# Scores and first mixing of a talking-heads attention as 64x32 TensorE tiles, with a new table of steps and two alternating orders of a step

## The chip, the cores and the metric

The kernel runs on one core of a Trainium2 chip. The metric is the device time of one execution in microseconds (us). The clock that TensorE was granted in the profiled execution was 0.994 of full speed on average.

## What is computed

Everything is 32-bit float. A batch of 8, 12 heads, 448 positions, 64 numbers a head. The scores of all heads are mixed by a 12x12 matrix before the softmax and mixed again by another one after it; then a Fourier mix and a feed-forward block of width 768 and 3072 follow.

```python
def _attn_ref(q, k, v, w_pre, w_post):
    scores = scale * np.matmul(q, k.transpose(0, 1, 3, 2))
    scores = np.einsum('bhij,hg->bgij', scores, w_pre)
    scores = scores - np.max(scores, axis=-1, keepdims=True)
    attn = np.exp(scores)
    attn = attn / (np.sum(attn, axis=-1, keepdims=True) + 1e-09)
    attn = np.einsum('bhij,hg->bgij', attn, w_post)
    return np.matmul(attn, v)

def _moe_ref(x, w_ch1, w_ch2):          # x: heads side by side, (8, 448, 768)
    u = x + np.real(np.fft.fft(np.fft.fft(x, axis=1), axis=2))
    un = (u - mean(u)) / np.sqrt(var(u) + 1e-06)
    return u + np.maximum(un @ w_ch1, 0.0) @ w_ch2
```

## The kernel before

There are two stages. `mix_phase` does attention and the Fourier mix, batch by batch, in about the first 812 us; `ffn_phase` does the feed-forward block, a seven-product scheme of half-size matrices, in the rest. The weights of the feed-forward block arrive as 64-bit floats and are turned into 32-bit ones on VectorE by a chain of small instructions (lines 229 to 261, "conversions" here). One such instruction is dealt out per step of the attention loop by `wts.deal(1)`.

The attention loop has 24 steps a batch, 192 in all. Step s does the second half of the work for row group T = s and the first half for T = s + 2 (`LM`), and fetches for T = s + 4 (`LG`). The pieces:

- **Scores** (`emit_qk`, L443). For 56 rows twice (`Sb` holds 124 rows), two heads at a time by x, two half blocks by y. A matmul takes 64 rows of q transposed as weights, 64x64 tiles, and streams 448 columns of k. Results lie in `ms` tiles of PSUM and are copied to `Sb` by ScalarE (L324). There are four `ms` buffers, which the other pieces use too.
- **Gather** (`emit_gather`, L459). Four DMAs on the SP queue bring the 12 heads of 5 rows onto 60 partitions, `Kr`, three buffers.
- **First mixing** (`emit_premix`, L469). Four matmuls, 60 rows by 64 columns of weights `kw1`, 448 columns streamed, into `mx`: two tiles, one buffer each.
- **Maximum and exponential** (`emit_max` L477 on VectorE, `emit_exp` L485 on ScalarE), each once for x = 0 and once for x = 1. The exponential also sums into `den`.
- **Scaling** (`emit_scale`). VectorE makes the reciprocal `rcp` (L493, L494), GpSimd multiplies `PP` by it (L496).
- **Second mixing** (`emit_postmix`, L506). Eight matmuls in 64x32 tiles, 448 columns, into `po`, one buffer; `emit_turn` (L517) transposes it on VectorE into `Pv`.
- **Second product** (`emit_av`, L533). 28 matmuls in 64x64 tiles with `v`, 120 columns; results are copied to `XT` by ScalarE.
- **The 128-wide blocks** ("full" in the code). Transposition of q and k (`emit_xpose`, L420; evicted to `qT` and `kT`), of `XT` (`emit_x`, L566), and the two products of the Fourier mix (`emit_z` L631, `emit_s2` L647, which updates `X` on VectorE, L658 and L660). Between them GpSimd does additions, the "folds" (L587 to L608).

In a 32-bit matmul TensorE makes two passes, so that each matmul above is two MATMUL and two LDWEIGHTS records in the profile.

The order on TensorE, VectorE, ScalarE and GpSimd is written by hand. For each step the loop at the end of `mix_phase` emits the pieces in one fixed order: first mixing, eviction of what is pending (`flush`), second mixing, maxima, exponentials, the second product if one is due, transposition of `po`, a conversion, scores if due, gather, scaling, deferred stores and folds, 128-wide blocks if due. When a piece falls due is in tables: `AT_T` for q's and k's transpositions, `AT_QK` scores, `AT_AV` second products, `AT_X`, `AT_Z`, `AT_S` the other 128-wide ones. `ENG` says which engine evicts what ("a" ScalarE, "d" VectorE). DMAs on SP follow as semaphores allow.

Of the kernel before, what the change touches and what calls it, by code (L numbers as in the profile page):

```python
# [10 lines left out]
F32 = mybir.dt.float32  # L11
# [65 lines left out]
AT_T = ((12, 10), (17, 16), (14, 18))  # L77
AT_L = ((-4, -3), (-2, -1), (0, 1), (2, 8), (12, 13), (14, 15))
AT_V = ((3, 4), (5, 6), (7, 7))
AT_QK = ((1, 2, 2), (0, 1, 2), (0, 1, 2), (0, 1, 2),  # L80
         (0, 1, 2), (0, 1, 2), (0, 1, 2), (0, 1, 2))
AT_AV = ((0, 2, 3), (1, 3, 5), (3, 4, 5), (1, 2, 3))
AT_X = (11, 20, 24, 29)
AT_Z = (38, 38, 41, 41)
AT_S = ((40, 44), (53, 55))

ENG = {("tr", "q", 4): "d", ("tr", "q", 3): "a", ("tr", "k", 4): "d",
       ("tr", "k", 3): "a", "QK": "aa", "AV": "aa", "X": "aa", "z": "a"}
# [196 lines left out]
def mix_phase(ctx, tc, rest, ident, q, k, v, w_pre, w_post, u_scr, u_rev, wts):  # L285
# [40 lines left out]
    def flush():  # L326
        while pend:
            pend.pop(0)[1]()
# [103 lines left out]
    def emit_qk(n, xx):  # L432
# [7 lines left out]
        for y in range(2):  # L440
            lo = r0 + MG * y
            for x in range(2):
                nc.tensor.matmul(  # L443
                    pss[x][64 * y:64 * y + r0 + 64 - lo, :S],
                    st["qT", xx][64 * x:64 * x + 64, y, lo:r0 + 64],
                    st["kT", xx][64 * x:64 * x + 64, y, :],
                    start=True, stop=True)
# [16 lines left out]
    def emit_premix(T):  # L464
        mx = [pmx.tile([P, 512], F32, name="mx", tag=f"mx{x}") for x in range(2)]
        Kr = steps[T]["Kr"]
        for x in range(2):
            for z in range(2):
                nc.tensor.matmul(mx[x][64 * z:64 * z + 64, :S],  # L469
                                 kw1[64 * x:64 * x + KR, :],  # L470
                                 Kr[64 * x:64 * x + KR, z, :], start=True, stop=True)
        steps[T]["mx"] = mx

    def emit_max(T):
        nmx = [psm.tile([P, 1], F32, name="nmx", tag=f"nmx{x}") for x in range(2)]
        for x in range(2):
            nc.vector.tensor_reduce(nmx[x][:, :], steps[T]["mx"][x][:, :S],  # L477
                                    axis=AX.X, op=ALU.max, negate=True)
        steps[T]["nmx"] = nmx

    def emit_exp(T):
        PP = ppp.tile([P, 2, S], F32, name="PP", tag="PP")
        den = psm.tile([P, 2], F32, name="den", tag="den")
        for x in range(2):
            nc.scalar.activation(PP[:, x, :], steps[T]["mx"][x][:, :S], ACTF.Exp,  # L485
                                 bias=steps[T]["nmx"][x][:, :],
                                 accum_out=den[:, x:x + 1])
        steps[T]["PP"], steps[T]["den"] = PP, den
# [260 lines left out]
    with tc.manual_schedule(engines={ET.PE, ET.DVE, ET.Activation, ET.Pool}):  # L749
        while s <= TOT - GS + AT_X[-1]:  # L750
            old = len(later)
            n = take("none", s)
            if 0 <= s + LM < TOT:
                emit_premix(s + LM)
            flush()
            if 0 <= s < TOT:
                emit_postmix(s)
            if 0 <= s + LM < TOT:
                emit_max(s + LM)
                emit_exp(s + LM)  # L760
            take("AV", s)
            if 0 <= s < TOT:
                emit_turn(s)
            if s >= 4:
                wts.deal(1)
            take("QK", s)
            if 0 <= s + LG < TOT:
                if any(e[2] is not None and e[2] <= (s + LG) // BS for e in pend):
                    flush()
                emit_gather(s + LG)  # L770
            if 0 <= s + LM < TOT:
                emit_scale(s + LM)
            for _ in range(old):
                later.pop(0)()
            for _ in range(min(len(folds), 1 if n and s > 3 else 2)):
                folds.pop(0)()
            take("full", s)
# [344 lines left out]
```

## Time and profile before

| what | us |
|---|---|
| median of 6 runs (2423.2 to 2429.62) | 2424.76 |
| the profiled execution | 2423.69 |
| its span, from the first to the last instruction | 2421.9 |

Busy time of the engines inside the attention stage, in two stretches of 100 us:

| from, to (us) | TensorE | VectorE | ScalarE | GpSimd |
|---|---|---|---|---|
| 100 to 200 | 99.9 | 77.4 | 73.4 | 81.2 |
| 600 to 700 | 98.2 | 78.3 | 67.8 | 73.8 |

Groups of instructions of the attention stage (line, engine, operation, tiles, shape, count; busy us, mean ns of one; idle time of the engine just before, and what ended most of it):

```profile
L469 PE MATMUL mx<-Kr,kw 60*64 60x448 f32 x1536 | 221.3, 553 | 6.5 <-DMA Kr<-Sb 4.6
L506 PE MATMUL po<-PP,kw 60*32 60x448 f32 x3072 | 188.7, 548 | 1.6 <-DVE rcp L493 1.6
L443 PE MATMUL ms<-kT,qT 64*64 64x448 f32 (+1 forms) x1536 | 189.4, 553 | 0.0
L477 DVE TENSOR_REDUCE nmx<-mx 128x1 f32<-128x448 f32 x384 | 222.3, 618 | 125.2 <-PE mx L469 123.0
L485 ACT ACTIVATE PP<-mx,nmx 128x448 f32<-128x448 f32 x384 | 240.0, 630 | 168.4 <-DVE nmx L477 156.2
L496 POOL TENSOR_SCALAR PP<-PP,rcp 128x448 f32<-128x448 f32 x384 | 240.6, 635 | 234.8 <-DVE rcp L494 101.7
```

The busy time of such a group is the union of its instructions' time, since several small tiles work side by side in TensorE: 1536 times 553 ns is 849 us, and 221.3 us of the span have such a matmul in them. In names like `60*64` the first number is the rows of the weights and the second the columns. The ends of matmuls are modelled, their starts are recorded; so distances are measured from start to start.

### The profile page before, as it was taken

What the parts mean: (1) busy time and instruction counts of PE and PEld (TensorE: products, weight loads), DVE (VectorE), ACT (ScalarE), POOL (GpSimd) and SP (SyncE); (2) the same over time, 40 slices, a digit from 0 to 9 for tenths busy, and PEclk for the clock granted to TensorE, in tenths of its full rate; (3) what the DMA queues carried; (4) which work ended last, traced back from release to release, by engine and by line L of the source; (5) the groups of instructions that cost most, each with busy time, mean ns of one, the idle gap of its engine ahead of it and who ended that gap; (6) DMA issues with size and microseconds to landing.
All of it is one profiled execution on the core that took longest, in us unless ns stands there. A gap on an engine that the chain in (4) does not pass through costs nothing.

```text
span 2421.9 us, 48510 instructions
## 1 busy us (share of the span) xinstructions
PE 2379.2 (98%) x18608; PEld 1553.3 (64%) x18608; DVE 1506.6 (62%) x3103; ACT 798.4 (33%) x2059; POOL 780.8 (32%) x1293
## 2 busy tenths in 40 slices
PE   7999999999999899999999999999999999999999
PEld 2445454454555477776777777777777777777776
DVE  3777778788787647785567356635665457533333
ACT  4777667676667542322111111111111110111110
POOL 3587877868676531120111011101110011000000
PEclk8999999999999999999999999999999999999999
DMA  6555554656554456346444444534442534343331
GB/s 151 176 182 160 179 171 155 197 161 194 165 164 147 163 199 215 126 149 234 145 137 153 143 147 134 159 116 168 145 149 98 200 127 146 121 169 112 118 117 53
DMA packets 168596, 372.10 MB, mean 154 GB/s; under 512 B 36750, under 2 KB 90022, under 8 KB 168366
## 3 DMA queue, kind: packets, MB, share of 16 engines
q1 hardware_dynamic: 129038, 260.22, 31.9%
q0 software_dynamic: 33760, 107.40, 14.9%
q8 instruction: 149, 2.44, 0.4%
q10 hardware_dynamic: 5568, 1.38, 0.3%
q14 instruction: 81, 0.66, 0.1%
HBM read 211.98 MB, written 74.34 MB: 118 GB/s over the span
## 4 chain that ended last, share of the span: by engine, by line
PE 94%; DMA 2%; SPq 1%; DVE 1%; ACT 1%; issue 0%; ACTq 0%; DVEq 0%
PE psP L946 18%; PE psP L1002 18%; PE psR L946 9%; PE psR L1002 9%; PE mx L469 7%; PE po L506 6%; PE ms L533 6%; PE ms L443 6%; PE psQ L1002 5%; PE psQ L946 4%; PE ms L647 2%; PE ms L420 2%; DMA Kr<-Sb 1%; PE ms L631 1%; SPq L459 1%; PE ms L566 1%
## 5 line engine op out<-in xcount | busy, mean ns | idle before, releaser
L946 PE MATMUL psP<-ub,w1t 128*128 128x256 f32 x2016 | 462.5, 379 | 0.0
L1002 PE MATMUL psP<-w2t,h 128*128 128x384 f32 x1344 | 460.9, 486 | 0.0
L946 PEld LDWEIGHTS psP<-ub,w1t 128*128 128x128 f32 x2016 | 382.8, 190 | 60.7
L207 POOL DMA_DIRECT2D raw<-in_moe_w_ch_dram x120 | 68.9, 574 | 924.5 <-DVE tmp L251 905.7
L1002 PEld LDWEIGHTS psP<-w2t,h 128*128 128x128 f32 x1344 | 254.4, 190 | 165.9
L496 POOL TENSOR_SCALAR PP<-PP,rcp 128x448 f32<-128x448 f32 x384 | 240.6, 635 | 234.8 <-DVE rcp L494 101.7
L477 DVE TENSOR_REDUCE nmx<-mx 128x1 f32<-128x448 f32 x384 | 222.3, 618 | 125.2 <-PE mx L469 123.0
L485 ACT ACTIVATE PP<-mx,nmx 128x448 f32<-128x448 f32 x384 | 240.0, 630 | 168.4 <-DVE nmx L477 156.2
L951 ACT COPY h<-psP 128x512 f32<-128x512 f32 x42 | 24.6, 585 | 764.4 <-PE psP L946 753.2
L1008 DVE TENSOR_TENSOR u<-u,psP 128x384 f32<-128x384 f32 x336 | 183.5, 552 | 141.3 <-PE psP L1002 139.2
L946 PE MATMUL psR<-ub,w1t 128*128 128x256 f32 x1008 | 231.3, 379 | 0.0
L1002 PE MATMUL psR<-w2t,h 128*128 128x384 f32 x672 | 230.5, 486 | 0.0
L469 PE MATMUL mx<-Kr,kw 60*64 60x448 f32 x1536 | 221.3, 553 | 6.5 <-DMA Kr<-Sb 4.6
L517 DVE STREAM_TRANSPOSE Pv<-po 128x896 f32<-128x896 f32 x192 | 212.8, 1108 | 15.6 <-PE po L506 13.2
L957 DVE TENSOR_TENSOR h<-h,psQ 128x512 f32<-128x512 f32 x42 | 28.9, 688 | 298.8 <-PE psQ L946 298.6
L946 PEld LDWEIGHTS psR<-ub,w1t 128*128 128x128 f32 x1008 | 191.4, 190 | 25.9
L324 ACT COPY Sb<-ms 124x448 f32<-124x448 f32 x384 | 184.7, 539 | 17.2 <-PE ms L631 5.1
L506 PE MATMUL po<-PP,kw 60*32 60x448 f32 x3072 | 188.7, 548 | 1.6 <-DVE rcp L493 1.6
L533 PEld LDWEIGHTS ms<-Pv,vv 64*64 64x64 f32 x5376 | 144.7, 133 | 70.1 <-issue 33.1
L443 PE MATMUL ms<-kT,qT 64*64 64x448 f32 (+1 forms) x1536 | 189.4, 553 | 0.0
L1002 PEld LDWEIGHTS psR<-w2t,h 128*128 128x128 f32 x672 | 127.2, 190 | 87.4
L533 PE MATMUL ms<-Pv,vv 64*64 64x120 f32 x5376 | 167.8, 269 | 0.9 <-issue 0.9
(92 smaller groups left out, 2753.0 us busy)
## 6 DMA issues: line engine op xcount, KB each, us to landing
ub<-ub SPq DMA_DIRECT2D x294, 384.0 KB
Kr<-Sb SPq DMA_DIRECT2D x768, 105.0 KB
raw<-in_moe_w_ch_dram POOLq DMA_DIRECT2D x72, 256.0 KB, 3.3
raw<-in_moe_w_ch_dram POOLq DMA_DIRECT2D x48, 384.0 KB, 3.7
w<-wst POOLq DMA_DIRECT2D x126, 128.0 KB, 3.0
w<-wst POOLq DMA_DIRECT2D x84, 192.0 KB, 3.1
w1t<-w SPq DMA_DIRECT2D x42, 384.0 KB
w2t<-w SPq DMA_DIRECT2D x42, 384.0 KB
```

Source lines behind the costliest of these rows:

```text
L324: (nc.scalar.copy if eng == "a" else nc.vector.tensor_copy)(out=out, in_=in_)
L443: nc.tensor.matmul(pss[x][64 * y:64 * y + r0 + 64 - lo, :S], st["qT", xx][64 * x:64 * x + 64, y, lo:r0 + 64], st["kT", xx][64 * x:64 * x + ...
L469: nc.tensor.matmul(mx[x][64 * z:64 * z + 64, :S], kw1[64 * x:64 * x + KR, :], Kr[64 * x:64 * x + KR, z, :], start=True, stop=True)
L477: nc.vector.tensor_reduce(nmx[x][:, :], steps[T]["mx"][x][:, :S], axis=AX.X, op=ALU.max, negate=True)
L485: nc.scalar.activation(PP[:, x, :], steps[T]["mx"][x][:, :S], ACTF.Exp, bias=steps[T]["nmx"][x][:, :], accum_out=den[:, x:x + 1])
L496: nc.gpsimd.tensor_scalar(PP[:, x, :], PP[:, x, :], rcp[:, x:x + 1], 1.0, op0=ALU.mult, op1=ALU.mult)
L506: nc.tensor.matmul(po[o:o + 32, z, :S], kw2[64 * z:64 * z + KR, y, :], PP[64 * z:64 * z + KR, :, c * HS:(c + 1) * HS], start=True, stop=True)
L517: nc.vector.transpose(g["Pv"][:, T % GT, :].rearrange("p (z s) -> p z s", z=2), steps[T]["po"][:, :, :S])
L533: nc.tensor.matmul(pss[y][64 * x:64 * x + 64, :nu * R], st["v", pr][64 * y:64 * y + 64, x, jb * D:(jb + 1) * D], _ap(Pv, 64 * y * rp + 32 ...
L946: nc.tensor.matmul(p[:, m, :], w1[i][:, kc, m * P:(m + 1) * P], ub[:, kc, :], start=i in OPENS and m == kc == 0, stop=kc == NK - 1, skip_g ...
L1002: nc.tensor.matmul(p, lhs[i][:, kf, x * P:(x + 1) * P], w2[i][:, kf, :], start=i in OPENS and kf == 0, stop=kf == FM - 1, skip_group_check ...
L1008: nc.vector.tensor_tensor(us_, us_, p, op=ALU.add)
```

## The change

The matmuls of the scores and of the first mixing are cut in two along the columns of their weights, 32 (or 28) each, with the output in partitions 32 further on. Maximum and exponential are emitted for x = 0 and x = 1 apart. The step's order is read from a table, one row for even and one for odd steps; in even steps the conversion comes first, and second product before scores; in odd steps scores come before the second product, and the conversion after scaling and gather. In both rows the pending evictions are emitted after the second mixing instead of before it, and the gather after the scaling (in even steps after the 128-wide blocks too). The tables of due times are changed, and the eviction of k's transposition swaps its two engines.

```diff
@@ -74,18 +74,24 @@
 
 
 
-AT_T = ((12, 10), (17, 16), (14, 18))
+AT_T = ((6, 10), (17, 18), (14, 16))
 AT_L = ((-4, -3), (-2, -1), (0, 1), (2, 8), (12, 13), (14, 15))
 AT_V = ((3, 4), (5, 6), (7, 7))
-AT_QK = ((1, 2, 2), (0, 1, 2), (0, 1, 2), (0, 1, 2),
+AT_QK = ((1, 2, 2), (0, 1, 2), (0, 1, 2), (1, 1, 2),
          (0, 1, 2), (0, 1, 2), (0, 1, 2), (0, 1, 2))
-AT_AV = ((0, 2, 3), (1, 3, 5), (3, 4, 5), (1, 2, 3))
+AT_AV = ((1, 2, 3), (0, 1, 5), (3, 4, 5), (1, 2, 4))
 AT_X = (11, 20, 24, 29)
-AT_Z = (38, 38, 41, 41)
-AT_S = ((40, 44), (53, 55))
-
-ENG = {("tr", "q", 4): "d", ("tr", "q", 3): "a", ("tr", "k", 4): "d",
-       ("tr", "k", 3): "a", "QK": "aa", "AV": "aa", "X": "aa", "z": "a"}
+AT_Z = (39, 39, 41, 41)
+AT_S = ((40, 44), (48, 54))
+
+ORDERS = tuple(o.split() for o in (
+    "conv pre post flush AV max0 exp0 "
+    "QK max1 exp1 turn scale full gather",
+    "pre post flush max0 max1 QK exp0 "
+    "AV turn exp1 scale gather conv full flush"))
+
+ENG = {("tr", "q", 4): "d", ("tr", "q", 3): "a", ("tr", "k", 4): "a",
+       ("tr", "k", 3): "d", "QK": "aa", "AV": "aa", "X": "aa", "z": "a"}
 
 
 
@@ -438,13 +444,15 @@
         r0 = bk["r0"]
         pss = [ms_tile() for _ in range(2)]
         for y in range(2):
-            lo = r0 + MG * y
-            for x in range(2):
-                nc.tensor.matmul(
-                    pss[x][64 * y:64 * y + r0 + 64 - lo, :S],
-                    st["qT", xx][64 * x:64 * x + 64, y, lo:r0 + 64],
-                    st["kT", xx][64 * x:64 * x + 64, y, :],
-                    start=True, stop=True)
+            for lo in (r0 + MG * y, r0 + MG * y + 32):
+                o = 64 * y + lo - r0 - MG * y
+                hi = min(lo + 32, r0 + 64)
+                for x in range(2):
+                    nc.tensor.matmul(
+                        pss[x][o:o + hi - lo, :S],
+                        st["qT", xx][64 * x:64 * x + 64, y, lo:hi],
+                        st["kT", xx][64 * x:64 * x + 64, y, :],
+                        start=True, stop=True)
         return [lambda x=x: copy(ENG["QK"][x], bk["Sb"][:124, 2 * xx + x, :],
                                  pss[x][:124, :S]) for x in range(2)]
 
@@ -466,26 +474,24 @@
         Kr = steps[T]["Kr"]
         for x in range(2):
             for z in range(2):
-                nc.tensor.matmul(mx[x][64 * z:64 * z + 64, :S],
-                                 kw1[64 * x:64 * x + KR, :],
-                                 Kr[64 * x:64 * x + KR, z, :], start=True, stop=True)
+                for o in (0, 32):
+                    nc.tensor.matmul(mx[x][64 * z + o:64 * z + o + 32, :S],
+                                     kw1[64 * x:64 * x + KR, o:o + 32],
+                                     Kr[64 * x:64 * x + KR, z, :], start=True, stop=True)
         steps[T]["mx"] = mx
 
-    def emit_max(T):
-        nmx = [psm.tile([P, 1], F32, name="nmx", tag=f"nmx{x}") for x in range(2)]
-        for x in range(2):
-            nc.vector.tensor_reduce(nmx[x][:, :], steps[T]["mx"][x][:, :S],
-                                    axis=AX.X, op=ALU.max, negate=True)
-        steps[T]["nmx"] = nmx
-
-    def emit_exp(T):
-        PP = ppp.tile([P, 2, S], F32, name="PP", tag="PP")
-        den = psm.tile([P, 2], F32, name="den", tag="den")
-        for x in range(2):
-            nc.scalar.activation(PP[:, x, :], steps[T]["mx"][x][:, :S], ACTF.Exp,
-                                 bias=steps[T]["nmx"][x][:, :],
-                                 accum_out=den[:, x:x + 1])
-        steps[T]["PP"], steps[T]["den"] = PP, den
+    def emit_max(T, x):
+        nmx = steps[T]["nmx", x] = psm.tile([P, 1], F32, name="nmx", tag=f"nmx{x}")
+        nc.vector.tensor_reduce(nmx[:, :], steps[T]["mx"][x][:, :S],
+                                axis=AX.X, op=ALU.max, negate=True)
+
+    def emit_exp(T, x):
+        if x == 0:
+            steps[T]["PP"] = ppp.tile([P, 2, S], F32, name="PP", tag="PP")
+            steps[T]["den"] = psm.tile([P, 2], F32, name="den", tag="den")
+        nc.scalar.activation(steps[T]["PP"][:, x, :], steps[T]["mx"][x][:, :S], ACTF.Exp,
+                             bias=steps[T]["nmx", x][:, :],
+                             accum_out=steps[T]["den"][:, x:x + 1])
 
     def emit_scale(T):
         PP, den = steps[T]["PP"], steps[T]["den"]
@@ -750,31 +756,33 @@
         while s <= TOT - GS + AT_X[-1]:
             old = len(later)
             n = take("none", s)
-            if 0 <= s + LM < TOT:
-                emit_premix(s + LM)
-            flush()
-            if 0 <= s < TOT:
-                emit_postmix(s)
-            if 0 <= s + LM < TOT:
-                emit_max(s + LM)
-                emit_exp(s + LM)
-            take("AV", s)
-            if 0 <= s < TOT:
-                emit_turn(s)
-            if s >= 4:
-                wts.deal(1)
-            take("QK", s)
-            if 0 <= s + LG < TOT:
-                if any(e[2] is not None and e[2] <= (s + LG) // BS for e in pend):
+            ahead, now = 0 <= s + LM < TOT, 0 <= s < TOT
+            for op in ORDERS[s % 2]:
+                if op == "flush":
                     flush()
-                emit_gather(s + LG)
-            if 0 <= s + LM < TOT:
-                emit_scale(s + LM)
-            for _ in range(old):
-                later.pop(0)()
-            for _ in range(min(len(folds), 1 if n and s > 3 else 2)):
-                folds.pop(0)()
-            take("full", s)
+                elif op in fill:
+                    take(op, s)
+                elif op == "conv":
+                    if s >= 4:
+                        wts.deal(1)
+                elif op == "gather":
+                    if 0 <= s + LG < TOT:
+                        if any(e[2] is not None and e[2] <= (s + LG) // BS for e in pend):
+                            flush()
+                        emit_gather(s + LG)
+                elif op == "scale":
+                    if ahead:
+                        emit_scale(s + LM)
+                    for _ in range(old):
+                        later.pop(0)()
+                    for _ in range(min(len(folds), 1 if n and s > 3 else 2)):
+                        folds.pop(0)()
+                elif op in ("post", "turn"):
+                    if now:
+                        (emit_postmix if op == "post" else emit_turn)(s)
+                elif ahead:
+                    (emit_premix if op == "pre" else emit_max if op[0] == "m"
+                     else emit_exp)(s + LM, *map(int, op[3:]))
             s += 1
         flush()
         wts.deal(1000)
```

## The prediction

> **What bounds the kernel now.** I read the slices of the page first, then the chain that ended last, then TensorE's timeline inside the attention stage, and last the waits of that stage.
>
> ```profile
> PE 2379.2 (98%) x18608; PEld 1553.3 (64%) x18608; DVE 1506.6 (62%) x3103; ACT 798.4 (33%) x2059; POOL 780.8 (32%) x1293
> ...
> PE   7999999999999899999999999999999999999999
> PE 94%; DMA 2%; SPq 1%; DVE 1%; ACT 1%; issue 0%; ACTq 0%; DVEq 0%
> ```
>
> TensorE is nearly always busy and is 94% of the chain. The change touches only the attention stage, about 30 to 812 us; the feed-forward lines L946 and L1002 that fill the rest stay as they are. So the question is what TensorE does in a step of the attention loop. Four lines of its timeline say it (start, length, engine, line, tiles, count):
>
> ```profile
> 503.30 0.98 PE L443 MATMUL ms<-kT,qT 64*64 64x448 f32 x8
> 504.05 0.98 PE L469 MATMUL mx<-Kr,kw 60*64 60x448 f32 x8
> 504.96 0.98 PE L506 MATMUL po<-PP,kw 60*32 60x448 f32 x16
> 505.87 0.98 PE L443 MATMUL ms<-kT,qT 64*64 64x448 f32 x8
> 506.78 1.56 PE L647 MATMUL ms<-tcs,z 97*112 97x193 f32 x8
> ```
>
> Read the starts, not the modelled lengths. Scores to first mixing, both in 64x64 tiles: 504.05 - 503.30 = 0.75 us. First mixing to second mixing, 64x64 to 64x32: 0.91. Second mixing to scores: 0.91. Scores to a 128-wide block: 0.91. I took all block-to-block starts from 60 to 790 us: scores to first mixing 0.750 (86 times, median), second mixing to anything 0.912 (173 times), scores to anything 128 wide 0.909, second product (L533) 1.509 before scores and 1.662 before a 128-wide block. So a block costs its streaming, and **0.16 us more if the next block has another tile shape**: 0.912 - 0.750 = 0.162 after a block of 448 columns, 0.16 after the second product, about 0.16 after a transposition of q or k (0.912 before the first mixing, against 0.75), 0.09 after L647 (1.494 against 1.401). Also, 16 instructions in 64x32 tiles (L506) take the same 0.912 as 8 in 64x64 tiles.
>
> What TensorE still waits for is small and sits at the first mixing. The waits from 100 to 800 us (who waited for whom, us in total, times, longest):
>
> ```profile
> ACT PP L485 <- DVE nmx L477: 129.3, 146, 3.1
> DVE nmx L477 <- PE mx L469: 96.5, 112, 1.6
> ```
>
> And one such place in the timelines of VectorE, GpSimd and TensorE:
>
> ```profile
> 585.75 0.96 DVE L493 TENSOR_SCALAR rcp<-den 128x2 f32<-128x2 f32 x1
> ...
> 585.48 1.21 POOL L592 TENSOR_TENSOR xs<-xs 113x383 f32<-113x383 f32 x1
> ...
> 588.90 1.58 PE L469 MATMUL mx<-Kr,kw 60*64 60x448 f32 x8 [0.38 <-ACT PP L485]
> ```
>
> mx has one buffer, so a first mixing can't run before the exponentials of the step before have read it. From one first mixing (500.00) the maximum starts at 501.02, the second exponential's accumulator read ends at 503.08: **a loop of 3.08 us** that a shorter step can't beat. When VectorE is late, so is the loop: the small L493, 0.16 us usually, took 0.96 beside the GpSimd operation above, and conversions grew from 0.52 to 1.88 (L261 at 583.94).
>
> **The change part by part.**
>
> *Scores and first mixing in 64x32 tiles.* Twice the instructions (4 to 8 matmuls, each two passes), same columns streamed. Not in the trace: two 64x32 blocks in a row. Bounds: 0.750 each, as 64x64 to 64x64 does and 128 to 128 does; 0.912 each, as if the small tiles always drained. I take 0.750, since in L506 the weights of the second pass are loaded within 0.03 us of the first pass's start, before it ends.
>
> A page speaks against this: the Trainium skill, TensorEngine Tiling (Array Packing), section Performance Considerations, gives each matmul an overhead of some 60 cycles. As an estimate from that page, 8 more instructions a block at 25 ns would be 0.2 us, over 384 blocks 77 us, and the sum below would turn to 44 us slower. The trace disagrees: L506's 16 instructions start some 7 ns apart and cost what 8 do.
>
> *How many shape changes go.* Counted in the instruction order of the two built programs up to the feed-forward part: 549 before, 346 after. By the block that is left: blocks of 448 columns 455 to 168 (first mixing 190 to 0, second mixing 192 to 49, scores 73 to 119), 287 x 0.162 = 46.5 us gained; second product 11 to 93, 82 x 0.157 = 12.9 us lost; blocks 128 wide 83 to 85, some 0.3 us lost. **Net 33.3 us.** A step with a second product gains nothing (4.08 to 4.07 us: two changes either way); one with a transposition goes 3.65 to 3.32, with L566 3.58 to 3.25.
>
> The same by batch of 24 steps. Before: 11 steps of 4.08 and, for the others, 5.28, 5.05, 6.03, 3.65 (three), 3.32, 4.98 (two), 3.58 (two), 2.57, 4.23: 99.4 us. After: 10 of 4.07, then 5.87, 4.15, 4.72 (two), 4.65 (two), 3.32 (four), 3.25 (two), 3.00 (two): 95.2. Measured before: first mixings five batches apart start at 196.58 and 712.48, 103.2 a batch, so **3.75 us of waits a batch**.
>
> *The waits with the new table and orders.* Before, one step in a batch was only 2.57 us long; the loop of 3.08 makes it wait 0.5. After, the shortest two have 3.00: 0.2 together. At the start of the stage seven steps of 2.25 us (2.57 before) can't use their 0.32: 2 us not gained, once. The other 3.2 us of waits come with late maxima. VectorE's part of a step: maxima 1.08, transposition of po 1.03, L493 and L494 0.37, conversion 0.25 to 0.5, and evictions (qT 1.09, kT 0.67, four L658/L660 1.9). The table spreads evictions out: before, a step with kT, one with L566 and one with qT, all of 3.6 us, followed each other once a batch (the wait at 588.90 is there); after, two steps of 4.07 lie between the second and the third. k's evictions swap halves between ACT and VectorE: 0.67 becomes about 0.5 on VectorE, 24 times, off the path. Against it: in odd steps the conversion is moved past the scaling's issue, and the next even step begins with one, so two conversions stand right behind L494, just when GpSimd starts its two L496 (1.25 us). If the second one waits for both, VectorE ends at 2.55 + 0.35 + 1.25 + 0.35 = 4.5 us after the odd step's maximum began, and the next maximum is late by 0.4 us after a step of 4.07, by 1.2 after one of 3.00. The following step hides its length less 3.08: 1.0 of a 4.07, 0.2 of a 3.32. So some 0.1 to 0.5 us remain in a few steps of a batch. Bounds for all late maxima: 1 us a batch (spread out, no stall) and 6 (every odd step 0.5); I take 3.4, near what it was, since the same conversions and folds meet in both.
>
> *Moved otherwise.* The gathers of Kr (four on SP, 0.77 us each, 3.07 a step) move behind the 128-wide blocks in even steps. Issue's end stood a median 4.8 us ahead of the first mixing that needs it, 2.2 at the lowest twentieth; a later place of under 1 us lies in that, and if it didn't, what is late next is L469, as in 18 waits of 7.3 us in all between 100 and 800 us. Behind the gathers on SP stand only u's stores. q's and k's loads on GpSimd change order only. The added loads of weights run beside matmuls (PEld is busy 0.2 us of a block).
>
> Sum against the profiled execution, 2423.7 us (span 2421.9): -33.3 + 2 - 8 x (0.3 less waiting in short steps, 0.2 more behind VectorE) = about -32, so 2391.6; that run was 1 us under the median, **2392** against the median.
>
> **Rivals.**
>
> *Waits take it back.* The two conversions behind L494 hit the scaling and folds in every odd step, and the maximum of the next even step is late beyond its slack. For: L493 grew up to 1.65 us beside GpSimd, VectorE is 78% busy in 100 to 200 us and would be 81%. Against: most odd steps are 4.07 long. It decides from 33/96 = 0.35 us a pair of steps on; at 0.5 us, 48 us: 2392 + 48 = 2440, slower. At half of this, 2416.
>
> *64x32 in a row drains all the same.* Then every 448-column block costs 0.912. After the change 408 of them are followed by their own shape: 408 x 0.162 = 66 us, 2458. For: never seen in the trace. Against: both other shapes run on without it.
>
> *More than the sum.* Late maxima fall to 1 us a batch: 8 x 2.4 = 19 us more, 2373.
>
> *The change doesn't do what it says* (shape changes that the hardware doesn't see as such, or steps bound elsewhere): 2424.
>
> **How the numbers follow.** Forecast (2380 to 2408): 0.70. More than the sum, below 2380: 0.12. Waits take it back: 0.11, of which half still under 2420. Draining all the same: 0.04. Nothing: 0.03. The range 2375 to 2411 leaves no more than 0.2 out. A run tells 0.2%, 4.8 us, from no change. Faster: 0.70 + 0.12 + 0.06 = 0.88; within: 0.03; slower: 0.09.
>
> **What would show it.** Right: first to second mixing, and second mixing to scores, 0.75 us from start to start; second product to first mixing 1.66; a batch of some 99 us; the stage ending near 780 instead of 812, and the feed-forward part as long as before. Wrong: 0.91 between 64x32 blocks (the second rival), or 0.75 with L478, the new line of the first mixing, stretched beyond 1.2 us in many steps and conversions of over 1 us ahead of them (the first).

## The result, and the profile after

| | before | after |
|---|---|---|
| median, us (lowest to highest; runs) | 2424.89 (2419.45 to 2430.46; 43) | 2416.7 (2411.53 to 2428.19; 21) |
| the profiled execution, us | 2423.69 | 2426.21 |
| its span, us | 2421.9 | 2424.4 |
| last start less first start of the feed-forward products (L946 and L1002; L954 and L1010) | 2417.5 - 866.5 = 1551.0 | 2420.0 - 869.1 = 1550.9 |

The ratio is 0.9968, 95% interval [0.996, 0.9976]: some 8 us faster, where 33 were forecast. One thing must be kept in mind in all that follows: the execution of the changed kernel that was profiled is one of its longer ones, 9.5 us above its median. The feed-forward part is as long as it was, so the shortfall lies in the attention stage.

The page of the changed kernel, the engines' busy time and the chain that ended last, by engine:

```profile
PE 2364.2 (98%) x21680; PEld 1595.9 (66%) x21680; DVE 1546.4 (64%) x3103; ACT 799.3 (33%) x2059; POOL 792.6 (33%) x1293
...
PE 87%; DMA 4%; POOL 3%; DVE 2%; SPq 2%; ACT 1%; issue 1%; ACTq 0%; DVEq 0%; POOLq 0%
```

TensorE is busy for 15 us less, and the span isn't shorter. Its share of the chain fell from 94% to 87%, and DMA's rose from 2% to 4%, GpSimd's to 3%. Busy time alone says that the change did its work; the chain says that other things came to set more of the time.

The groups that answer to those of before (columns as there):

```profile
L478 PE MATMUL mx<-Kr,kw 60*32 60x448 f32 x3072 | 230.7, 549 | 16.9 <-DMA Kr<-Sb 13.9
L512 PE MATMUL po<-PP,kw 60*32 60x448 f32 x3072 | 211.1, 542 | 4.1 <-POOL PP L502 2.2
L451 PE MATMUL ms<-kT,qT 64*32 64x448 f32 (+1 forms) x3072 | 203.7, 547 | 0.7 <-DVE wrp L366 0.7
L485 DVE TENSOR_REDUCE nmx<-mx 128x1 f32<-128x448 f32 x384 | 222.6, 617 | 104.8 <-PE mx L478 102.6
L492 ACT ACTIVATE PP<-mx,nmx 128x448 f32<-128x448 f32 x384 | 240.2, 630 | 173.7 <-DVE nmx L485 162.5
L502 POOL TENSOR_SCALAR PP<-PP,rcp 128x448 f32<-128x448 f32 x384 | 253.7, 670 | 225.1 <-DVE rcp L500 181.7
```

The first mixing (L478) idles 16.9 us where it idled 6.5, nearly all of it for `Kr`. The scaling (L502) is a little longer, and 181.7 us of its idle time are put down to the reciprocal instead of 101.7; in all it idles less (225.1 us, 234.8 before).

Four lines of TensorE's timeline after, where nothing is late (start, length, engine, line, tiles, count):

```profile
301.07 0.98 PE L478 MATMUL mx<-Kr,kw 60*32 60x448 f32 x16
301.84 0.96 PE L512 MATMUL po<-PP,kw 60*32 60x448 f32 x16
302.60 0.96 PE L451 MATMUL ms<-kT,qT 64*32 64x448 f32 x16
303.49 1.56 PE L653 MATMUL ms<-tcs,z 97*112 97x193 f32 x8
```

From start to start: 0.77, 0.76, and 0.89 before the 128-wide block. Over the whole stage the medians are 0.752 from second mixing to scores, 0.776 from first to second mixing, and 0.890 before another shape. Before, all three were 0.91. So the saving is there, block by block: all of it between blocks of 448 columns, a little even at a change of shape.

Where a part of it went shows in what the first mixing waited for, from 100 to 780 us. Before (who released it; us in total, times):

```profile
  ACT PP L485: 13.1, 33
  DMA Kr<-Sb: 7.4, 18
```

After:

```profile
  DMA Kr<-Sb: 25.8, 25
...
  ACT PP L492: 13.6, 45
```

The wait for the fetch has grown by 18.4 us, and the wait for the exponentials, the loop that the prediction looked at, has hardly grown. These sums take in the idle time of the weight loads (PEld), which run beside the matmuls of the block before, so they are not all time that TensorE lost. Taken apart (longest in the last place), before:

```profile
PEld mx L469 <- DMA Kr<-Sb: 6.6, 16, 1.2
PE mx L469 <- DMA Kr<-Sb: 0.8, 2, 0.4
```

After:

```profile
PEld mx L478 <- DMA Kr<-Sb: 19.2, 19, 3.9
PE mx L478 <- DMA Kr<-Sb: 6.6, 6, 3.1
```

One of the 25 in TensorE's timeline:

```profile
558.03 1.71 PE L451 MATMUL ms<-kT,qT 64*32 64x448 f32 x32
559.54 1.04 PE L478 MATMUL mx<-Kr,kw 60*32 60x448 f32 x12
563.66 0.96 PE L478 MATMUL mx<-Kr,kw 60*32 60x448 f32 x2 [3.08 <-DMA Kr<-Sb]
563.78 0.99 PE L512 MATMUL po<-PP,kw 60*32 60x448 f32 x6
564.41 0.96 PE L478 MATMUL mx<-Kr,kw 60*32 60x448 f32 x2
564.49 2.37 PE L512 MATMUL po<-PP,kw 60*32 60x448 f32 x10
```

Twelve of the sixteen matmul records of the first mixing run; the rest stand 3.08 us for the last of the four fetches. The chain of this place (start, length, what) names it:

```profile
554.17 0.77 SPq L467
554.98 0.77 SPq L467
555.79 7.83 DMA Kr<-Sb
```

SP issues one fetch after the other, and from 555.79 to 563.62 the chain does nothing but wait for one of them to land. Then look at the last of the six lines of the timeline: after the wait ten records of the second mixing take 2.37 us, where sixteen took 0.96. The stretch there (from:to, length, busy us and count of TensorE, weight loads, VectorE, ScalarE and GpSimd, granted clock, DMA share, GB/s) tells why:

```profile
562.00:570.00 8.00, 6.33 (x84) 3.57 (x92) 4.04 (x6) 1.64 (x5) 4.72 (x9) 0.57 0.57 152
```

The granted clock is 0.57. Between 100 and 780 us the clock records of this execution hold three windows at half speed, at 354 us (3.4 us long), 464 (3.4) and 563 (6.8); the records of before hold none there. Each begins about the end of a wait of TensorE of 2.3 to 3.1 us (from 1.0 us before to 0.6 us after it), two of them for `Kr`, one for GpSimd's setting of columns of `XT` to zero (L561). The Trainium skill, TensorE: Matmul & The Clock Gate, Part 1, has the clock halved after an idle window of some 3.4 us; here waits of 2.3 us by the profile were enough. They need not be: a wait of 2.32 us in a3 and one of 2.86 in b1 (runs described below) have no such window behind them.

**The account.** For the six batches from first mixing 24 to first mixing 168, TensorE's own work is summed with the prediction's block times in program order; what is left of the measured time is waits and lost clock:

| profiled execution | measured | work | left over | first mixing (weight loads and matmuls) waits for `Kr`, 100 to 780 us |
|---|---|---|---|---|
| before | 615.3 | 593.3 | 22.0 | 7.4 |
| after | 615.6 | 569.0 | 46.6 | 25.8 |

The work is 24.3 us less and the rest 24.6 us more. What the 24.6 are is counted from start to start: the time from a block's last matmul start to the next block's, less the lower quartile of this time for the same pair of blocks. By the block that comes late, before and after: first mixing 18.8 and 31.0 us, transposition of `XT` 0.5 and 5.3, second mixing 0.1 and 5.2, second product 3.6 and 7.3. Of the first mixing's part, the fetch delays TensorE by 7.1 us before and 19.1 after, the exponentials by 9.4 and 4.7. So the fetch is about half of the 24.6, and the other half is spread over waits for ScalarE and GpSimd. The half clock is in these figures: its windows take 13.6 us, in which some 6 us of work are lost.

Outside these batches the two profiled executions nearly balance: first mixing 0 starts 3.4 us later after the change, first mixing 0 to 24 takes 2.4 us more, and from first mixing 168 to the last it is 3.2 us less. In a run at the median, 9.5 us shorter, some 15 of the 24.6 remain, if all of the difference lies here. Whether a usual execution of the changed kernel loses more to the clock than one of before isn't shown: the mean granted clock over the whole span is 0.995 in both (23 and 84 executions).

### The profile page after: what moved, and what is told of

It is laid out like the page before. It is cut to its first block, busy times and chain, and to the rows that moved or that the text cites. A ratio compares the mean times of both kernels' runs of the same rounds, so it can differ in the third digit from the quotient of the medians.

```text
span 2424.4 us, 54667 instructions
## 1 busy us (share of the span) xinstructions
PE 2364.2 (98%) x21680; PEld 1595.9 (66%) x21680; DVE 1546.4 (64%) x3103; ACT 799.3 (33%) x2059; POOL 792.6 (33%) x1293
## 4 chain that ended last, share of the span: by engine, by line
PE 87%; DMA 4%; POOL 3%; DVE 2%; SPq 2%; ACT 1%; issue 1%; ACTq 0%; DVEq 0%; POOLq 0%
PE psP L954 18%; PE psP L1010 18%; PE psR L954 9%; PE psR L1010 9%; PE mx L478 6%; PE ms L451 5%; PE ms L539 5%; PE psQ L1010 5%; PE psQ L954 4%; PE po L512 4%; DMA Kr<-Sb 3%; PE ms L653 2%; SPq L467 1%; PE ms L426 1%; PE ms L637 1%; POOL PP L502 1%
## 5 line engine op out<-in xcount | busy, mean ns | idle before, releaser
L954 PE MATMUL psP<-ub,w1t 128*128 128x256 f32 x2016 | 462.6, 379 | 0.0
L1010 PE MATMUL psP<-w2t,h 128*128 128x384 f32 x1344 | 460.9, 486 | 0.0
L954 PEld LDWEIGHTS psP<-ub,w1t 128*128 128x128 f32 x2016 | 382.8, 190 | 60.7
L1010 PEld LDWEIGHTS psP<-w2t,h 128*128 128x128 f32 x1344 | 254.4, 190 | 165.9
L502 POOL TENSOR_SCALAR PP<-PP,rcp 128x448 f32<-128x448 f32 x384 | 253.7, 670 | 225.1 <-DVE rcp L500 181.7
L959 ACT COPY h<-psP 128x512 f32<-128x512 f32 x42 | 24.6, 585 | 764.4 <-PE psP L954 753.2
L478 PE MATMUL mx<-Kr,kw 60*32 60x448 f32 x3072 | 230.7, 549 | 16.9 <-DMA Kr<-Sb 13.9
L954 PE MATMUL psR<-ub,w1t 128*128 128x256 f32 x1008 | 231.3, 379 | 0.0
L1010 PE MATMUL psR<-w2t,h 128*128 128x384 f32 x672 | 230.5, 486 | 0.0
L512 PE MATMUL po<-PP,kw 60*32 60x448 f32 x3072 | 211.1, 542 | 4.1 <-POOL PP L502 2.2
L954 PEld LDWEIGHTS psR<-ub,w1t 128*128 128x128 f32 x1008 | 191.4, 190 | 25.9
L451 PE MATMUL ms<-kT,qT 64*32 64x448 f32 (+1 forms) x3072 | 203.7, 547 | 0.7 <-DVE wrp L366 0.7
L539 PEld LDWEIGHTS ms<-Pv,vv 64*64 64x64 f32 x5376 | 146.5, 134 | 73.4 <-issue 35.1
L330 ACT COPY Sb<-ms 124x448 f32<-124x448 f32 x384 | 183.8, 541 | 29.6 <-DMA Kr<-Sb 13.6
L1010 PEld LDWEIGHTS psR<-w2t,h 128*128 128x128 f32 x672 | 127.2, 190 | 87.4
```

Of the source, the lines that this page charges most:

```text
L330: (nc.scalar.copy if eng == "a" else nc.vector.tensor_copy)(out=out, in_=in_)
L451: nc.tensor.matmul(pss[x][o:o + hi - lo, :S], st["qT", xx][64 * x:64 * x + 64, y, lo:hi], st["kT", xx][64 * x:64 * x + 64, y, :], start=Tr ...
L478: nc.tensor.matmul(mx[x][64 * z + o:64 * z + o + 32, :S], kw1[64 * x:64 * x + KR, o:o + 32], Kr[64 * x:64 * x + KR, z, :], start=True, sto ...
L502: nc.gpsimd.tensor_scalar(PP[:, x, :], PP[:, x, :], rcp[:, x:x + 1], 1.0, op0=ALU.mult, op1=ALU.mult)
L512: nc.tensor.matmul(po[o:o + 32, z, :S], kw2[64 * z:64 * z + KR, y, :], PP[64 * z:64 * z + KR, :, c * HS:(c + 1) * HS], start=True, stop=True)
L539: nc.tensor.matmul(pss[y][64 * x:64 * x + 64, :nu * R], st["v", pr][64 * y:64 * y + 64, x, jb * D:(jb + 1) * D], _ap(Pv, 64 * y * rp + 32 ...
```

## The experiments

My theory was that the shape drain is real and that two things take its gain back: the conversions in their new place, and the chain from scores over the copy to `Sb` and the fetch to the first mixing. Times are medians; each ratio is to the kernel before, on the same chip. "Left over" and "waits for `Kr`" are the columns of the account, from the one execution that was profiled: in a1 it is 7 us above the median, in b2 5.5, in the change 9.5, in the others it is within 4.5 of it, so differences of a few us in these columns decide nothing.

### Tiles alone, order alone, tiles with the new tables

Three parts of the change. `a1_tiles_only` is the kernel before with only the two hunks of `emit_qk` and `emit_premix`. `a2_order_only` is the change without them:

```diff
-                for o in (0, 32):
-                    nc.tensor.matmul(mx[x][64 * z + o:64 * z + o + 32, :S],
...
+                nc.tensor.matmul(mx[x][64 * z:64 * z + 64, :S],
```

`c3_tiles_tables` has tiles, tables and `ENG`, and the old loop in place of `ORDERS`.

> The kernel before with the 64x32 tiles alone: old tables, old order of a step. The shape changes by block are the same 33.3 us fewer as in the whole change. Theory K (the fetch of Kr can't follow shorter steps): some 10 to 18 us faster than before, since the 17 steps with neither a second product nor a 128-wide block now wait 0.83 us each for the loop of 3.08 instead of 0.51 (5 us lost). Theory P (the new places of the conversions cost the time): the old places are kept here, so at least 25 us faster than before, under 2400. A third reading, that 64x32 blocks in a row don't run on, would give no gain.

> The whole change with the old 64x64 tiles in scores and first mixing: new tables, ENG and orders alone. Theory P: slower than before by 15 to 25 us, all of what the change gave back. Theory K: steps are as long as before and the fetch follows, so within 5 us of before, perhaps a little faster since no step is shorter than 3.08 us in a batch.

> The 64x32 tiles with the new tables and ENG, but the old order in every step (the conversion between transposition and scaling, scores always after the second product). If the new tables are what helps a3 over a1: as a3, 0.989 to 0.992. If it is the two alternating orders: as a1, 0.996 to 0.998.

| | ratio [95%] | us | left over | waits for `Kr` |
|---|---|---|---|---|
| a1_tiles_only | 0.997 [0.9951, 0.9988] | 2421.38 | 46.0 | 26.9 |
| a2_order_only | 1.0006 [0.9996, 1.0017] | 2430.72 | 26.1 | 10.3 |
| c3_tiles_tables | 1.0006 [0.9994, 1.0018] | 2430.01 | 56.2 | 46.0 |
| the change | 0.9968 [0.996, 0.9976] | 2416.7 | 46.6 | 25.8 |

Counted in TensorE's timeline, the tiles alone have 345 shape changes and the change 347 (551 before); their TensorE work is the same within 0.5 us, and so is their gain. So tables and orders could only have been worth something by way of the waits, and as they stand they brought nothing: the new tables with the old order are worse than the tiles alone, and the first mixing then waits 46 us for `Kr`.

### Half of each fetch

`a4_half_gather` is the change with two of the four DMAs, `b2_half_cols` with four of half the length, `b3_tiles_half` is a1 with two DMAs, and `c1_before_half`, the control, is the kernel before with two. They leave out half of what is fetched; TensorE's work is as long.

```diff
-        for z in range(2):
+        for z in range(1):
             for x in range(2):
...
-                                     Kr[64 * x:64 * x + KR, z, :], start=True, stop=True)
+                                     Kr[64 * x:64 * x + KR, 0, :], start=True, stop=True)
```

> The whole change, but only two of the four DMAs of a gather are issued, and the first mixing reads their half of Kr for both z: half of the fetched rows is left out of the computation, TensorE's work is as long. Theory K: Kr lands 1.5 us sooner after its scores are there, and the DMA queues carry 40 MB less, so 15 to 25 us faster than the whole change, near 2395. Theory P: within 5 us of the whole change.

> The whole change with all four DMAs of a gather, each of 224 instead of 448 columns; the first mixing reads these twice (half of the columns is left out of the computation). SP issues as long as in the change, the bytes are those of a4. If the time that SP takes to issue four DMAs is what makes Kr late: within 5 us of the whole change, ratio to before 0.995 to 0.999. If bytes and the queueing of the transfers are: as a4, 0.985 to 0.989.

> The tiles alone (a1: old tables, old order) with half of the gathers (half of the fetched rows is left out). If the fetch of Kr is also what took back most of a1's gain: 15 us or more faster than a1, ratio to before near 0.989, and the new tables and orders were not needed to get there. If a1 lost it to the loop of maximum and exponential: 0.994 to 0.997.

> The kernel before with half of the gathers (half of the fetched rows is left out), a control for a4, b1 and b3. If its longer steps hid the fetch of Kr: within 5 us of before, 0.998 to 1.000; then the gain of b3 over a1 belongs to the shorter steps. If half the fetch is worth something by itself: 0.985 to 0.990, and only the rest can be put to the change.

| | ratio [95%] | us | against its own full fetch | left over |
|---|---|---|---|---|
| a4_half_gather | 0.9869 [0.9847, 0.9891] | 2398.2 | -24 | 34.2 |
| b2_half_cols | 0.9883 [0.9867, 0.9899] | 2399.19 | -21 | 32.1 |
| b3_tiles_half | 0.9822 [0.9808, 0.9835] | 2383.49 | -36 | 22.8 |
| c1_before_half | 0.9886 [0.9872, 0.9901] | 2402.51 | -28 | 10.7 |

(The fourth column is the difference of the ratios times 2425.) Four readings. First, b2 is nearly as good as a4, though SP issues as many DMAs as in the change: for the most part the bytes count, not the issue. Only from first mixing 0 to 24 does the issue show, by 81.3 us in a4, 88.4 in b2 and 96.1 in the change. Second, with the fetch out of the way the tiles bring 0.9822 against 0.9886, 16 us, double of what they brought with it. Third, the control fell out against me: I had held that the kernel before hides its fetch, and it gains 28 us by half of it as well. About 9 of them lie in the first 24 steps (93.7 to 84.4 us), the others in the later batches. So the kernel before stood at the edge of this chain already.

Fourth, and against my theory again: the change with half the fetch (0.9869) is 4 us ahead of the control (0.9886), within the noise, where with the whole fetch it was 8 ahead of before. Its left over is 34.2 against 10.7, 23.5 more, as with the whole fetch (24.6 more). So the 24 us that a4 gains say nothing of the shortfall: the kernel before gains as much. With the fetch out of the way other pieces come late instead: in a4's profile the transposition of `XT` by 13.2 us in all, from start to start. Only for the tiles alone does the fetch explain a part of what was missing: with half of it they bring 16 us of the 33 instead of 8.

What is next when the fetch is gone, in b3, from 100 to 780 us at the first mixing:

```profile
  ACT PP L488: 35.1, 70
```

It is the loop through the one buffer of `mx`: 13.1 us before, 35.1 here. From start to start the exponentials delay TensorE by 18.7 us in b3 and 11.4 in c1; b3's left over is 12.1 us above c1's, so this loop is more than half of what b3 lacks to the 33.

### The conversions

`a3_conv_back` takes the conversion behind the transposition of `po` again, in both orders. `b1_half_conv_back` is that with two DMAs. `e1_no_conv` is the change with four of the seven VectorE instructions of each conversion replaced by `pass`.

```diff
-    "conv pre post flush AV max0 exp0 "
-    "QK max1 exp1 turn scale full gather",
+    "pre post flush AV max0 exp0 "
+    "QK max1 exp1 turn conv scale full gather",
     "pre post flush max0 max1 QK exp0 "
-    "AV turn exp1 scale gather conv full flush"))
+    "AV turn conv exp1 scale gather full flush"))
```

> The whole change, but the conversion stands behind the transposition of po in both orders, as before the change. Theory P: 15 to 25 us faster than the whole change, near 2395. Theory K: within 5 us of the whole change, 2412 to 2420.

> Half of the gathers (as in a4; half of the fetched rows is left out) and the conversions in their old place (as in a3) together. If the fetch of Kr and the conversions are two separate losses, the gains add: against the whole change 15 and 24 us, ratio to before near 0.981. If both runs shortened the same waits, no more than a4 alone: 0.986 to 0.988.

> The whole change with four of the seven VectorE instructions of each conversion left out (clamp, sign, power and lower; the feed-forward weights are therefore not the right numbers); loads, stores and the pace of dealing stay. If the conversions' meeting with GpSimd's operations is what the new places cost: as a3 or a little faster, ratio to before 0.986 to 0.991. If a3's gain over the change came from the order of the other pieces: within 5 us of the change, 0.995 to 0.998.

| | ratio [95%] | us | left over | waits for `Kr` |
|---|---|---|---|---|
| a3_conv_back | 0.9905 [0.9883, 0.9927] | 2406.49 | 30.7 | 19.0 |
| b1_half_conv_back | 0.9829 [0.9814, 0.9844] | 2386.26 | 20.6 | none |
| e1_no_conv | 0.9945 [0.9927, 0.9964] | 2417.71 | 43.5 | 29.2 |

a3 beats both kernels: 0.9905 against 0.9968 is 15 us for moving one short instruction of each step, and a3 is 23 us faster than before. With half the fetch the same move is worth 0.9869 to 0.9829, 10 us. The wait of GpSimd for the reciprocal (who waits for whom; us, times, longest; 100 to 780 us), first the change:

```profile
POOL PP L502 <- DVE rcp L500: 134.8, 79, 4.4
...
POOL PP L502 <- ACT Sb L330: 3.7, 5, 2.2
```

and a3:

```profile
POOL PP L502 <- DVE rcp L500: 85.1, 53, 4.2
POOL PP L502 <- ACT Sb L330: 47.5, 34, 3.8
```

The wait is mostly put down to another engine: with all releasers the scaling waits 151.1 us in the change, 144.3 in a3 and 163.8 before, so this wait isn't what the move saves. On VectorE the new place does what the prediction's first rival feared: from 100 to 780 us the conversions take 91.1 us in the change, 78.9 in a3 and 72.1 before, and in even steps a tenth of the first maxima start more than 2.4 us after the first mixing, 1.1 in a3 (2.0 before). But that hardly reaches TensorE by the way the rival took: from start to start the exponentials delay the first mixing by 4.7 us in the change and 4.1 in a3. And leaving out more than half of the conversions' time (91.1 to 42.0 us) gains only 6 us (0.9968 to 0.9945, with intervals that overlap) and leaves the wait for `Kr` where it was, so it isn't the conversions' own length alone. Nor is it the small instructions' meeting with GpSimd: the two-element instruction of L499, summed from 60 to 800 us, exceeds its usual 0.17 us by some 26 us in the change and 25 in a3 (15 before).

What a3 has less in the account is waits for `Kr` (from start to start 14.3 us of delay instead of 19.1) and, in that stretch, all of the 13.6 us at half clock. One thing points at why, without being a test: from issue's end to landing, the 95th percentile of the fetches is 5.6 to 5.8 us in the three kernels with whole fetches and conversions in the new places (the change, a2, e1), and 4.5 to 5.4 in the nine others that fetch whole and on SP alone. e1 keeps the loads and stores of the conversions, which share the DMA engines with the fetches. How the moved conversion saves 15 us isn't settled.

### The order of scores and second product

`d1_qk_first` gives a3's odd row to every step. `d2_tiles_qk_first` and `d3_before_qk_first` are a1 and the kernel before with the two exchanged:

```diff
-            take("AV", s)
+            take("QK", s)
             if 0 <= s < TOT:
                 emit_turn(s)
             if s >= 4:
                 wts.deal(1)
-            take("QK", s)
+            take("AV", s)
```

`c2_conv_back_qk` is a3 with the scores of one part of a block due a step earlier: `(0, 1, 2)` becomes `(0, 1, 1)` in the third entry of `AT_QK`.

> a3 with the odd order in every step: scores always ahead of the second product, conversion behind the transposition of po. Shape changes as in the change (two for a step with a second product either way). If the fetch behind the scores is the chain that binds, scores that end 1.5 us earlier in the 30 even steps with both help: 4 to 10 us faster than a3, ratio to before 0.986 to 0.989. If it is not: as a3, or slower by the copies of the second product that now come later, 0.990 to 0.994.

> a1 (tiles alone, old tables and order) with scores and second product swapped in the step and nothing else. If the place of the scores is what separates a3 from a1 and c3: 8 to 17 us faster than a1, ratio to before 0.990 to 0.994. If it is something else in the two orders (when the pending copies are emitted, where the gather stands): as a1, 0.996 to 0.998.

> The kernel before with the same swap and the old 64x64 tiles. The second product and the scores have the same tiles there, so TensorE's work stays. If before waits for the fetch too, as c1 says: 3 to 10 us faster than before. If only the shorter steps wait for it: 0.998 to 1.001.

> a3 with the last scores of the third block of a batch one step earlier (AT_QK's third entry 0, 1, 1), so that its gather has three steps instead of two of 3.3 and 3.0 us; TensorE's work stays the same, all is computed. In a3 this row group's Kr lands a median 1.7 us after the first mixing could start, 8 times. Theory K: 5 to 12 us faster than a3, 0.986 to 0.989. If the waits only move to the next block: 0.990 to 0.991.

| | ratio [95%] | us | waits for `Kr` |
|---|---|---|---|
| d1_qk_first | 0.9928 [0.9911, 0.9945] | 2407.62 | 16.9 |
| d2_tiles_qk_first | 0.9947 [0.9928, 0.9965] | 2412.37 | 13.4 |
| d3_before_qk_first | 0.9973 [0.9962, 0.9983] | 2419.23 | 13.4 |
| c2_conv_back_qk | 0.9926 [0.9912, 0.9939] | 2413.42 | 10.5 |

Scores 1.5 us earlier are worth 6.5 us without the tiles (d3), and with them 0.997 to 0.9947, 6 us, though these intervals overlap. d2's wait for `Kr` is half of a1's 26.9. d1 can't be told from a3, so that the alternation itself is worth nothing that shows; but d1 is 19 us ahead of c3, which differs from it in the order of a step alone, and c3 waits 29 us longer for `Kr`. So the new order has its worth beside the new tables: it makes up for what they lose. c2 and d3 are misses in part. c2's earlier scores moved waits rather than removed them: the wait for `Kr` falls from 19.0 to 10.5 us, but the transposition of `XT` is held up by GpSimd for 9.6 us (2.4 in a3), and the time is no better (0.9926 against 0.9905, intervals that overlap). In d3's profiled execution, the longest of its twelve, the wait for `Kr` is longer than in that of before (13.4 against 7.4), though the median is 6.5 us lower; what it saves isn't found. Both show that the wait for `Kr` alone doesn't foretell the time.

### Two attempts that made it slower

`b4_conv_back_act` is a3 with two of the four fetches of a block's first step issued by ScalarE, right behind its copy to `Sb`. `e2_post_first` is a3 with the second mixing ahead of the first.

```diff
-                nc.sync.dma_start(
+                (nc.scalar if T % BS == 0 and z else nc.sync).dma_start(
```

```diff
-    "pre post flush AV max0 exp0 "
+    "post pre flush turn AV max0 exp0 "
```

> a3 (conversions in their old place) with two of the four DMAs of the first gather of a block of scores issued by ScalarE, right behind its own copies, instead of by SP; all is computed. If Kr comes late by SP's issuing: 5 to 12 us faster than a3, ratio to before 0.986 to 0.989. If ScalarE's 1.3 us for the two issues, once in three steps, delay its copies and exponentials as much: as a3 or slower, 0.990 to 0.994.

> a3 with the second mixing ahead of the first one in every step, and the transposition of po ahead of the maxima; all is computed, shape changes as in a3 (345). It gives the fetch 0.75 us more and takes 0.75 us from the scaling, which L512 waits for. If late fetches are the larger loss that is left in a3: 5 to 15 us faster than a3, 0.984 to 0.988. If the scaling is then late as often: 0.990 to 0.996.

b4: 1.0035 [1.0012, 1.0058], 2433.42 us. e2: 1.0057 [1.0042, 1.0072], 2441.87 us. Both were meant to shorten the chain to the first mixing, and are 32 and 37 us slower than a3. The waits of b4 from 100 to 780 us:

```profile
PEld mx L478 <- DMA Kr<-Sb: 32.3, 27, 3.8
...
PE mx L478 <- DMA Kr<-Sb: 15.3, 13, 3.0
```

47.6 us for `Kr` where a3 has 19.0: the two fetches that leave ScalarE start a median 4.5 us after the last scores' last matmul, against 4.3 from SP in a3, and a tenth of them after more than 6.4 us, against 5.1. ScalarE's copies and exponentials stand behind them. In e2 the fetch has what it was to have, 6.9 us of waits for it, and another loop is late, by its waits:

```profile
ACT PP L492 <- DVE nmx L485: 200.1, 145, 3.4
...
DVE rcp L499 <- ACT PP L492: 65.7, 104, 1.0
```

The transposition of `po` stands ahead of the maximum on VectorE there, so what the first mixing gains is, it seems, paid for in maximum, exponential and scaling.

## Why the prediction went wrong

**Right: the shapes.** 64x32 blocks run on in one another (0.75 to 0.78 where 0.91 was), double scores take 1.506, and 346 shape changes instead of 549 are worth about what was said: the account's 24.3 us for six batches of eight. The rival "64x32 in a row drains all the same" is out, and so is the overhead per matmul that was weighed there: a block of 16 records takes the time that a block of 8 took. Feed-forward part: unchanged, as said.

**Right: what isn't gained at the start.** "2 us not gained" there was too little: from first mixing 0 to 24 it is 93.7 before and 96.1 after, so nothing of some 4 us was gained. Not the loop of 3.08 sets those steps, but the fetches, as half of them shows (84.4 before, 81.3 after).

**Wrong: the step on the waits.** For late maxima the prediction said "I take 3.4, near what it was", and its sum has "0.2 more behind VectorE" a batch, 1.6 us in all, in which the conversions' new place is counted. a3 measures that place: 15 us. It is the one term that an experiment shows to be wrong, and it is more than half of the 25 us between forecast and result. With the conversions back the kernel is 23 us faster than before; the other 10 us of the 33 are waits too (left over 30.7 in a3, 22.0 before), in the profile most of all for the fetch (14.3 us of delay against 7.1), though half the fetch doesn't give them back (b1 is 14 us ahead of its control c1). All waits and lost clock per batch, forecast as 3.6, went from 22.0/6 = 3.7 to 46.6/6 = 7.8 in the profiled executions, beyond the upper bound of 6 that was set for the late maxima; at the median it is some 6, if the difference lies there.

The gather's "a later place of under 1 us lies in that" failed as well. Two errors lie in it.

The first is how the slack was measured. "Issue's end stood a median 4.8 us ahead of the first mixing" leaves out the landing. From 100 to 780 us, issue's end to landing takes 2.7 us at the median in both, but 4.5 before and 5.8 after at the 95th percentile, and up to 7.4 and 7.5. Counted to the landing of the last of the four fetches, the lowest twentieth had no slack even before: -0.9 us, that is, it landed after the first mixing's first weight load; after it is -1.3, and the worst went from -1.7 to -4.45. The 18 waits of 7.3 us that the prediction quoted were the sign that this chain was already tight, and not a small remainder.

The second is what such a chain does when TensorE gets faster. The last scores of a block start 9.75 us before the first mixing that needs them, 10.0 after the change (medians); copy, issue and transfer in between don't shorten with TensorE's blocks. The steps that cover them do, by 0.33 us where they have no second product. So a late fetch costs more after. That is argued from these times; what was tested is that with half the fetch the tiles alone bring 16 us instead of 8, and the whole change 4 instead of 8.

**The first rival** ("waits take it back", at half price 2416) ends at the measured time, but that is luck as far as its mechanism goes. It had the right cause, the conversions' new place, and late maxima in even steps are there; but its way from there to TensorE, the exponentials at the first mixing, takes 4.7 us after where it took 9.4 before. **More than the sum** had nothing for it.

**Still open.** How the conversions' place costs its 15 us; what it costs with the old tiles, where tables and orders with the conversions back were not run; and a third buffer of `Sb` or a fourth of `Kr`, which wasn't tried.

## What to carry to other kernels

Where one engine is busy for 98% of the time, as here, its shortening is worth no more than the slack of the other chains, and that slack is to be counted to the landing of a transfer, and at its lowest twentieth rather than its median. Moving a short instruction on another engine can cost more than the change brings: try it by itself (a3). To learn what a chain costs, shorten it in both kernels and compare the gains: half the fetch made the change 24 us faster, which looked like the cause until it made the kernel before 28 us faster. And the idle time that a profile gives for weight loads is not time that TensorE lost.

## What the runs showed of the hardware

- Half clock within a stage at 97% busy (the change, 100 to 780 us): windows of 3.4 and 6.8 us about the end of waits of 2.3 to 3.1 us. Over all 18 profiles, in that stretch, each of the 8 waits of TensorE of 3.0 us or more has such a window that begins within some 2 us of its end; of the 7 waits from 2 to 3 us 4 have one, of the 22 from 1.5 to 2 us also 4.
- Over 23 executions of the changed kernel the time falls by 1.7 us for each 0.001 of mean granted clock (correlation -0.78): 2428.2 us at 0.989, 2411.5 to 2416.2 at 0.997 and 0.998. In the kernel before it is -0.2 over 84 executions.
- A shape change after 448 columns in 64x32 tiles costs 0.890 - 0.752 = 0.14 us, a little less than the 0.162 after 64x64 tiles.
- A DMA from SBUF to SBUF of 105 KB that lands in 2.7 us at the median takes up to 7.5 us in the same loop, from issue's end to landing (the change; 7.4 before).
